# Tile 1 of the MoE in mixed blocks: its h units all move into the third MoE stage, and two h units leave the place ahead of the third column

## The chip, the cores and the metric

The kernel runs on one core of one Trainium2 chip. The metric is the device time of one execution in microseconds (us), as a median over runs. The engines are called TensorE (PE, with PEld for its weight loads), VectorE (DVE), ScalarE (ACT), GpSimd (POOL) and SyncE (SP, which here only issues DMAs). POOL issues DMAs too.

## The reference

For each of 8 batches, attention without softmax gates `u`, and the result goes through a two-layer block with activation h·cos(h):

```python
scores = (1 / S) * z @ z.T            # z: 3008 x 64 for each batch
attn = np.maximum(scores, 0.0) ** 2
x = u * (attn @ v)                    # u, v: 3008 x 256
h = x @ w_in                          # 256 x 2048
out = (h * np.cos(h)) @ w_out         # 2048 x 256
```

Inputs and output are float32; the kernel computes in fp16 with float32 sums.

## The kernel before

The tokens of a batch are cut into 6 columns of 512 (the last has 448), so there are 48 tiles or slots, numbered by s = 6·batch + column. Each slot has two stages, and the main loop runs them in turn: `phase_a(s)` is the attention of column s, `phase_b(s)` the MoE of earlier tiles. The first three columns use `phase_a_first`. All instructions are put out in an order written by hand; each engine and each DMA queue works through its own in that order and waits on semaphores.

- **Scores** (`emit_score`, matmuls at L191): a 128x1024 block into one of three PSUM buffers E, which rotate. ScalarE takes the relu into r (L204), VectorE squares it into a piece A (L209, L212). Half of the pieces come from their mirror image by a DMA transpose on SP's queue (L244; L238 for those on the diagonal). Scores are put out ahead of need, between the value matmuls.
- **Values** (`emit_value`, L258): v times A. The first half of the features is summed in the two banks M, the second half in one buffer E. `gate_sum` copies one bank on ScalarE (L269) and adds the other on VectorE (L270); with that the bank or the buffer is free. `gate_mul` (L286) multiplies with the transposed u (uT) and gives x: the first half on VectorE inside `phase_a(s)`, the second on POOL at the head of `phase_b(s)`. In `phase_a_first` the two products of a tile are made later: those of tile 0 and 1 inside the next column on VectorE, those of tile 2 on POOL at the head of `phase_b(2)`. x has two buffers, so tile 3 takes that of tile 1.
- **h units** (`emit_h(m, i)`, i = 0 to 7): four matmuls of 512 columns (L403) into a buffer E, the cosine on ScalarE (L411, the profile's c), and h·cos(h) on VectorE (L414), which gives g and frees E. g has two buffers.
- **y, plain** (`emit_y(m, i)`, L507): eight matmuls of 256 columns into the two banks M; eight such steps make a tile. `store_y` evicts with ScalarE (L537).
- **y, mixed blocks** (`product(m, n)`, L465): a Strassen-like form with 7 products of 16 matmuls of 128 columns, in place of the 8 steps. Before it, for each of the units 4 to 7, `mix_early` on POOL makes one sum and one difference of halves of g (L427, L428), and `mix_late` on VectorE makes s2 and s4 in four operations (L433, L435) inside the next `phase_a`. After each product its bank M is taken by ScalarE (L484) or VectorE (L478). Two more sums run on POOL: c12 after product 6 (L487) and c22 after product 7 (L490). VectorE's sum after product 3 reads c12, that after product 4 writes c21, which c22 reads. `mixed(m)` says which tiles take this form. The weights for it, w_mix, are made once on POOL (L444).

`phase_b(s)` makes the h units of tile s - 1 and the y of tile s - 2, in turns: one h unit, one step or product of y. The start differs: tile 0 has four h units ahead of column 2, its others and six units of tile 1 come in `phase_b(2)`, and the last two of tile 1 open `phase_b(3)`. The order of products is

```python
order_y = (5, 1, 6, 7, 2, 3, 4)
...
acc = M[order_y.index(n) % 2][:, 0:T]
```

Around this, POOL's queue holds, in order: `hold` (a one-element copy, L345, that waits for the sums of the column), the load of u for the next tile, w_out (L684, behind the hold of column 1), then after column 2 the loads of u(3), u(4) and the first half of z of batch 1 (L118, L124), w_mix, the gating of tile 2, the mixing of `phase_b(2)` if there is any, and after `phase_b(2)` the second half of z. There is one z16 buffer, so this second load waits for the transpose of the first half (L133), which stands on SP's queue behind the transposes of A and the stores of tile 0.

Of the kernel before, what the change touches and what calls it, by code (L numbers as in the profile page):

```python
# [14 lines left out]
def kernel(  # L15
# [18 lines left out]
    CW = 512  # L34
# [4 lines left out]
    NSLOT = B * NC  # L39
# [186 lines left out]
    def emit_turns(due, more=0):  # L226
        while turns and (turns[0][0] <= due or more > 0):
            if turns[0][0] > due:
                more -= 1
            (b, c), key = turns.pop(0)  # L230
            b, J, I = key
            i = turn_slots[key]
            a = piece_bufs[i]
            if I == J:
                a4 = a.rearrange("p (k w) -> p k w", w=CW)
                for rr in range(2, 4):
                    rows = P if J * 4 + rr < NB - 1 else H
                    nc.sync.dma_start_transpose(  # L238
                        a4[:, 0:2, rr * P:rr * P + rows],
                        a[0:rows, rr * CW:rr * CW + 2 * P],  # L240
                    )
            else:
                d = new_piece((b, I, J))
                nc.sync.dma_start_transpose(d.rearrange("p (n j) -> p n j", j=P), a)  # L244
            if pending.pop(i) == "dropped":
                free_pieces.append(i)
# [26 lines left out]
    def gate_mul(s, dh, sm, eng=None):  # L273
        eng = eng or nc.vector
        J = s % NC
        b = s // NC
        W = width(J)
        if s not in xs:
            if J == NC - 1 and b % 2 == 1:
                xs[s] = xodd  # L280
            else:
                xs[s] = xpool.tile([P, 2, CW], FP16, name="x")
        x = xs[s]
        uT = uTs[s].rearrange("p (k d) j -> p k d j", d=2)
        nk = W // P
        eng.tensor_tensor(  # L286
            x[:, dh, 0:nk * P].rearrange("p (k j) -> p k j", j=P),
            sm[:, 0:nk * P].rearrange("p (k j) -> p k j", j=P),
            uT[:, 0:nk, dh, :],
            ALU.mult,  # L290
        )
        if nk < 4:
            dst = x[:, dh, nk * P:W] if b % 2 == 1 else xodd[:, dh, W:CW]
            eng.tensor_tensor(
                dst, sm[:, nk * P:W], uT[:, nk, dh, 0:W - nk * P], ALU.mult
            )
# [8 lines left out]
    def phase_a(s):  # L305
# [11 lines left out]
        for i, (dh, k) in enumerate(steps):  # L317
            if dh == 2:
                emit_value(b, J, k, 0, 0, M[0], False, True)
                emit_value(b, J, k, 1, 1, acc1[1], True, False)  # L320
                gate(s, 0, M[0], M[1])
            else:
                acc = M if dh == 0 else acc1
                last = k == NB - 2
                for t in range(2):
                    emit_value(
                        b, J, k, t, dh, acc[t],
                        k == 0 and not (dh == 1 and t == 1),
                        last and not (dh == 0 and t == 0),
                    )  # L330
                if dh == 1 and (k % 4 == 3 or last):
                    drop_piece((b, J, k // 4))
            for _ in range(at.get(i, 0)):
                emit_score()
                emit_turns(divmod(s + 1, NC), 1)
            if i in mix_at and mixed(s - 2):
                mix_late(s - 2, *mix_at[i])
# [55 lines left out]
    def mwidth(m):  # L393
        return 3 * P if m % (2 * NC) == NC - 1 else CW

    def emit_h(m, i):
        W = mwidth(m)
        x = xs[m]
        e = E[take_e()]
        for f in range(2):  # L400
            ft = 2 * i + f
            for k in range(2):
                nc.tensor.matmul(  # L403
                    e[:, f, 0:W],
                    w_in16[:, k, ft * P:(ft + 1) * P],
                    x[:, k, 0:W],
                    start=(k == 0),
                    stop=(k == 1),
                )
        c = cpool.tile([P, 2, CW], FP16, name="c")  # L410
        nc.scalar.activation(c[:, :, 0:W], e[:, :, 0:W], AF.Sin, bias=half_pi, scale=inv_s2)  # L411
        if m not in gs:
            gs[m] = gpool.tile([P, NFT, CW], FP16, name="g")
        return lambda: nc.vector.scalar_tensor_tensor(  # L414
            gs[m][:, 2 * i:2 * i + 2, 0:W], e[:, :, 0:W], 1.0, c[:, :, 0:W], ALU.mult, ALU.mult
        )

    def mixed(m):
        return 2 <= m < NSLOT - 2 and mwidth(m) == CW

    F = NFT // 2
    T = 2 * P
# [1 line left out]
    def mix_early(m, j):  # L424
        g, f = gs[m], slice(2 * j, 2 * j + 2)
        lower = slice(F + 2 * j, F + 2 * j + 2)
        nc.gpsimd.tensor_tensor(s1[:, f, :], g[:, f, T:], g[:, lower, T:], ALU.add)  # L427
        nc.gpsimd.tensor_tensor(g[:, f, T:], g[:, f, 0:T], g[:, f, T:], ALU.subtract)  # L428
# [86 lines left out]
    def emit_y(m, i):  # L515
        for ft in range(2 * i, 2 * i + 2):
            for k in range(mwidth(m) // P):
                y_block(m, ft, k)

    def store_half(m, half, o):  # L520
        b, J = m // NC, m % NC
        n = min(2, mwidth(m) // P - 2 * half)
        t0 = b * S + J * CW + half * T
        if J == NC - 1 and half == 1 and n == 2:
            nc.sync.dma_start(out[t0:t0 + P, :], o[:, 0, :])
            nc.sync.dma_start(out[t0 + P:t0 + P + H, :], o[0:H, 1, :])
            nc.sync.dma_start(out[b * S - H:b * S, :], o[H:P, 1, :])
        else:
            nc.sync.dma_start(
                out[t0:t0 + n * P, :].rearrange("(k p) d -> p k d", p=P), o[:, 0:n, :]  # L530
            )

    def store_y(m):
        for half in range(2):
            n = min(2, mwidth(m) // P - 2 * half)
            o = opool.tile([P, 2, D], FP32, name="o")
            nc.scalar.activation(  # L537
                o[:, 0:n, :],
                M[half].rearrange("p (k d) -> p k d", d=D)[:, 0:n, :],
                AF.Copy, bias=0.0, scale=inv_s2,  # L540
            )
            store_half(m, half, o)
# [22 lines left out]
    def phase_b(s):  # L565
        y, hs = s - 2, [(s - 1, i) for i in (0, 4, 1, 5, 2, 6, 3, 7)]
        if s == 2:
            hs = [(0, i) for i in range(4, 8)] + [(1, i) for i in range(6)]
        elif s == 3:
            hs = [(1, 6), (1, 7)] + hs  # L570
        elif s == NSLOT + 1:
            hs = []
        for dh in range(len(late_sums)):
            gate_mul(s, 2 - len(late_sums), late_sums.pop(0), nc.gpsimd)
        if mixed(y):
            ys = [lambda n=n: product(y, n) for n in order_y]
        else:
            ys = [lambda i=i: emit_y(y, i) for i in range(8)]
            if len(hs) == 8:
                six, seven = ys[6:]  # L580
                ys[6:] = [lambda: (six(), seven(), store_y(y))]
            else:
                ys[7] = lambda f=ys[7]: (f(), store_y(y))
        n = 0
        for i, (m, unit) in enumerate(hs):
            times_c = emit_h(m, unit)
            if not mixed(y):
                times_c()
            if i < len(ys):
                ys[i]()  # L590
            if mixed(y):
                times_c()
            if mixed(m) and unit >= 4:
                mix_early(m, unit - 4)
            if i in (1, 3, 5):
                emit_turns((0, 0), 1)
# [85 lines left out]
    phase_a_first(0, 12, {4: lambda: turn_late(4), 8: lambda: turn_late(5)})  # L682
    phase_a_first(1, 12)
    nc.gpsimd.dma_start(w_out16, moe_w_out.rearrange("(k p) f -> p k f", p=P))  # L684
    for i in range(4):
        emit_h(0, i)()
    phase_a_first(2, 14)
    assert done_groups[0] == need[3]
# [3 lines left out]
    load_z(1, 0)  # L692
    mix_weights()
    phase_b(2)
    turn_z(1, 0)
    load_z(1, 1)
# [56 lines left out]
```

## Time and profile before

| | us |
|---|---|
| median of 3 runs | 1202.3 |
| lowest and highest | 1202.19, 1202.38 |
| profiled execution | 1201.01 |
| its span | 1199.2 |
| TensorE busy (matmuls) | 1188.9 |
| VectorE, ScalarE, POOL busy | 989.6, 796.2, 642.9 |

The granted TensorE clock of the profiled run is 0.999 of full speed. The stages at the start lie as follows in its span, by the first TensorE instruction of each: `phase_a_first(2)` 41.90, `phase_b(2)` 56.20, `phase_a(3)` 72.47, `phase_b(3)` 83.78, `phase_a(4)` 101.65, `phase_b(4)` 113.52, `phase_a(5)` 126.78. In a timeline row the columns are start, length, engine, line, operation, output <- input, count, and in brackets the idle time of that engine before it with what ended it. A waits row gives total us, times, longest.

### The profile page before, as it was taken

What the parts mean: (1) busy time and instruction counts of PE and PEld (TensorE: products, weight loads), DVE (VectorE), ACT (ScalarE), POOL (GpSimd) and SP (SyncE); (2) the same over time, 40 slices, a digit from 0 to 9 for tenths busy, and PEclk for the clock granted to TensorE, in tenths of its full rate; (3) what the DMA queues carried; (4) which work ended last, traced back from release to release, by engine and by line L of the source; (5) the groups of instructions that cost most, each with busy time, mean ns of one, the idle gap of its engine ahead of it and who ended that gap; (6) DMA issues with size and microseconds to landing.
All of it is one profiled execution on the core that took longest, in us unless ns stands there. A gap on an engine that the chain in (4) does not pass through costs nothing.

```text
span 1199.2 us, 28321 instructions
## 1 busy us (share of the span) xinstructions
PE 1188.9 (99%) x11695; PEld 703.2 (59%) x11695; DVE 989.6 (83%) x1248; ACT 796.2 (66%) x923; POOL 642.9 (54%) x657
## 2 busy tenths in 40 slices
PE   9999999999999999999999999999999999999998
PEld 4455655665556655665556655665556555666566
DVE  6858888888988887788988889788888888878775
ACT  7957666666766666666766676666766667666444
POOL 3155735567555571665746656166565765525440
PEclk9999999999999999999999999999999999999999
DMA  9999898869997589946999569983798837964301
GB/s 158 167 165 147 126 154 114 122 102 132 131 124 121 105 135 158 129 80 119 140 145 132 82 111 148 165 114 76 113 163 149 117 71 117 172 112 89 62 19 54
DMA packets 467410, 145.13 MB, mean 121 GB/s; under 512 B 391760, under 2 KB 467024, under 8 KB 467280
## 3 DMA queue, kind: packets, MB, share of 16 engines
q1 hardware_dynamic: 368304, 110.11, 52.8%
q0 software_dynamic: 97440, 32.78, 28.7%
q8 instruction: 91, 1.49, 0.5%
q10 hardware_dynamic: 1536, 0.43, 0.2%
q14 instruction: 39, 0.32, 0.1%
HBM read 66.32 MB, written 24.64 MB: 76 GB/s over the span
## 4 chain that ended last, share of the span: by engine, by line
PE 96%; ACT 1%; DVE 1%; issue 1%; DVEq 0%; ACTq 0%
PE E L403 27%; PE M L465 21%; PE M L258 20%; PE E L258 19%; PE E L191 5%; PE M L507 4%; ACT r L204 1%; DVE g L414 0%; PE E L636 0%; DVE A L209 0%; DVE sm L270 0%; DVE A L212 0%; PE E L507 0%; DVE x L286 0%; PE M L660 0%
## 5 line engine op out<-in xcount | busy, mean ns | idle before, releaser
L411 ACT ACTIVATE c<-E 128x1024 f16<-128x1024 f32 (+1 forms) x384 | 386.0, 1007 | 223.8 <-PE E L403 222.9
L414 DVE SCALAR_TENSOR_TENSOR g<-E,c 128x1024 f16<-128x1024 f32 (+1 forms) x384 | 458.9, 1197 | 77.5 <-ACT c L411 77.0
L204 ACT ACTIVATE r<-E 128x512 f16<-128x512 f32 (+1 forms) x342 | 327.9, 967 | 114.8 <-PE E L191 109.9
L258 PEld LDWEIGHTS <-v 64*128 64x128 f16 x4512 | 225.3, 94 | 252.3 <-issue 19.2
L403 PE MATMUL E<-x,w_in 128*128 128x512 f16 (+1 forms) x1408 | 354.3, 374 | 2.7 <-DVE sm L270 2.0
L258 PE MATMUL M<-A,v 64*128 64x512 f16 (+1 forms) x2256 | 282.9, 372 | 0.3 <-DVE sm L270 0.3
L427 POOL TENSOR_TENSOR s<-g 128x512 f16<-128x512 f16 x160 | 187.2, 1170 | 174.4 <-DVE g L414 132.6
L258 PE MATMUL E<-A,v 64*128 64x512 f16 (+1 forms) x2256 | 278.0, 372 | 0.0
L428 POOL TENSOR_TENSOR g<-g 128x512 f16<-128x512 f16 x160 | 198.2, 1239 | 12.6
L403 PEld LDWEIGHTS <-w_in 128*128 128x128 f16 x1536 | 134.6, 98 | 112.4 <-issue 22.7
L209 DVE TENSOR_TENSOR A<-r 128x1024 f16<-128x1024 f16 x240 | 172.6, 730 | 21.3 <-ACT r L204 20.6
L286 POOL TENSOR_TENSOR x<-sm,uT 128x512 f16<-128x512 f32 (+1 forms) x43 | 48.5, 1130 | 244.8 <-DVE sm L270 244.6
L465 PEld LDWEIGHTS <-g 128*128 128x128 f16 x2560 | 156.4, 98 | 36.1
L465 PEld LDWEIGHTS <-s 128*128 128x128 f16 x1920 | 117.3, 98 | 27.1
L191 PE MATMUL E<-zT 64*128 64x512 f16 (+2 forms) x684 | 126.6, 363 | 2.0 <-DVE zT L631 1.1
L433 DVE TENSOR_TENSOR s<-s,g 128x1024 f16<-128x1024 f16 x80 | 90.9, 1137 | 2.1 <-POOL s L427 2.1
L212 DVE TENSOR_TENSOR A<-r 128x512 f16<-128x512 f16 (+1 forms) x102 | 77.0, 756 | 15.0 <-ACT r L204 14.5
L465 PE MATMUL M<-w_out,g 128*128 128x128 f16 x1280 | 84.5, 219 | 0.0
L465 PE MATMUL M<-w_mix,s 128*128 128x128 f16 x1280 | 84.5, 219 | 0.0
L465 PE MATMUL M<-w_mix,g 128*128 128x128 f16 x1280 | 84.5, 219 | 0.0
L191 PEld LDWEIGHTS <-zT 64*128 64x128 f16 x684 | 35.7, 94 | 41.8 <-issue 4.1
L507 PE MATMUL M<-w_out,g 128*128 128x256 f16 x432 | 55.8, 273 | 0.4 <-DVE sm L270 0.4
(55 smaller groups left out, 685.6 us busy)
## 6 DMA issues: line engine op xcount, KB each, us to landing
out_dram<-o SPq DMA_DIRECT2D x87, 256.0 KB, 2.2
v<-in_v_dram POOLq DMA_DIRECT2D x40, 256.0 KB, 9.3
u<-in_u_dram POOLq DMA_DIRECT2D x40, 256.0 KB, 4.8
A<-A SPq DMA_TRANSPOSE x207, 5.4
z<-in_z_dram POOLq DMA_DIRECT2D x14, 192.0 KB, 11.3
z<-in_z_dram POOLq DMA_DIRECT2D x14, 176.0 KB, 6.0
v<-in_v_dram POOLq DMA_DIRECT2D x8, 192.0 KB, 12.2
u<-in_u_dram POOLq DMA_DIRECT2D x8, 192.0 KB, 4.0
```

The source lines that it names most:

```text
L191: nc.tensor.matmul(e[:, t, 0:W], zT[t * H:(t + 1) * H, k * P:(k + 1) * P], zT[t * H:(t + 1) * H, J * CW:J * CW + W], start=True, stop=True,)
L204: nc.scalar.activation(r[:, :, 0:W], e[:, :, 0:W], AF.Relu)
L209: nc.vector.tensor_tensor(a4, r4, r4, ALU.mult)
L258: nc.tensor.matmul(bank[:, 0:width(J)], vs[b, k // 4][t * H:(t + 1) * H, k % 4, dh * P:(dh + 1) * P], value_rhs(b, J, k, t), start=start, ...
L403: nc.tensor.matmul(e[:, f, 0:W], w_in16[:, k, ft * P:(ft + 1) * P], x[:, k, 0:W], start=(k == 0), stop=(k == 1),)
L411: nc.scalar.activation(c[:, :, 0:W], e[:, :, 0:W], AF.Sin, bias=half_pi, scale=inv_s2)
L414: return lambda: nc.vector.scalar_tensor_tensor(gs[m][:, 2 * i:2 * i + 2, 0:W], e[:, :, 0:W], 1.0, c[:, :, 0:W], ALU.mult, ALU.mult)
L427: nc.gpsimd.tensor_tensor(s1[:, f, :], g[:, f, T:], g[:, lower, T:], ALU.add)
L428: nc.gpsimd.tensor_tensor(g[:, f, T:], g[:, f, 0:T], g[:, f, T:], ALU.subtract)
L433: nc.vector.tensor_tensor(s2[:, f, :], s1[:, f, :], g[:, f, 0:T], ALU.subtract)
L465: nc.tensor.matmul(acc[:, k * P:(k + 1) * P], left[:, ft, k * P:(k + 1) * P], right[:, ft, :], start=(ft == 0 and k == 0), stop=(ft == F - ...
L507: nc.tensor.matmul(y_bank(m, k), gs[m][:, ft, k * P:(k + 1) * P], w_out16[:, ft, :], start=(ft == 0 and (k % 2 == 0 or (final and k == 3)) ...
```

## The change

Tile 1 joins the tiles that take mixed blocks. All eight of its h units stand in `phase_b(2)`, in the order 0, 4, 1, 5, 2, 6, 3, 7 in which the other tiles have theirs, behind h(0,2) to h(0,7). Only h(0,0) and h(0,1) stay ahead of `phase_a_first(2)`. With 14 h units there, the eight y steps of tile 0 follow the h units with the indices 1, 2, 4, 5, 7, 8, 10, 11 (counted from 0). `phase_b(3)` has the eight units of tile 2 alone, and the seven products of tile 1. For the other stages the new list of places gives the order that they had.

```diff
     def mixed(m):
-        return 2 <= m < NSLOT - 2 and mwidth(m) == CW
+        return 1 <= m < NSLOT - 2 and mwidth(m) == CW
...
         y, hs = s - 2, [(s - 1, i) for i in (0, 4, 1, 5, 2, 6, 3, 7)]
         if s == 2:
-            hs = [(0, i) for i in range(4, 8)] + [(1, i) for i in range(6)]
-        elif s == 3:
-            hs = [(1, 6), (1, 7)] + hs
-        elif s == NSLOT + 1:
-            hs = []
+            hs = [(0, i) for i in range(2, 8)] + hs
...
             ys = [lambda i=i: emit_y(y, i) for i in range(8)]
-            if len(hs) == 8:
-                six, seven = ys[6:]
-                ys[6:] = [lambda: (six(), seven(), store_y(y))]
-            else:
-                ys[7] = lambda f=ys[7]: (f(), store_y(y))
-        n = 0
+            ys[7] = lambda f=ys[7]: (f(), store_y(y))
+        n = len(hs)
+        if n > 8:
+            after = (1, 2, 4, 5, 7, 8, 10, 11)
+        elif mixed(y):
+            after = range(7)
+        else:
+            after = (0, 1, 2, 3, 4, 5, 6, 6)
         for i, (m, unit) in enumerate(hs):
             times_c = emit_h(m, unit)
             if not mixed(y):
                 times_c()
-            if i < len(ys):
-                ys[i]()
+            for f, place in zip(ys, after):
+                if place == i:
+                    f()
             if mixed(y):
                 times_c()
...
-    for i in range(4):
+    for i in range(2):
         emit_h(0, i)()
     phase_a_first(2, 14)
```

## The prediction, made before the result was known

> **What bounds the kernel now.** I read the page's busy times first, then the waits of TensorE, then the timeline around the places that the diff touches, then two stretches side by side.
>
> ```profile
> PE 1188.9 (99%) x11695; PEld 703.2 (59%) x11695; DVE 989.6 (83%) x1248; ACT 796.2 (66%) x923; POOL 642.9 (54%) x657
> ...
> PE E L403 <- DVE sm L270: 2.0, 1, 2.0
> PE E L403 <- DVE g L414: 0.7, 1, 0.7
> PE E L191 <- DVE g L414: 0.5, 1, 0.5
> PE M L507 <- DVE sm L270: 0.4, 1, 0.4
> ```
>
> TensorE works 99% of the span, and nearly all of its waits after the first 15 us are these four, each happening once, all before 90 us. So only two things can make this kernel shorter: fewer matmul columns, or the loss of one of these waits. The largest, 2.0 us, is here:
>
> ```profile
> 85.53 1.03 PE L403 MATMUL E<-x,w_in 128*128 128x512 f16 x4
> 86.59 0.69 DVE L286 TENSOR_TENSOR x<-sm,uT 128x512 f16<-128x512 f32 x1 [6.82 <-PE E L403]
> 88.67 0.68 DVE L270 TENSOR_TENSOR sm<-E,sm 128x512 f32<-128x512 f32 x1
> 89.41 1.02 PE L403 MATMUL E<-x,w_in 128*128 128x512 f16 x4 [1.98 <-DVE sm L270]
> ```
>
> [...] The gating product of tile 3 (L286, in phase_a(3)) stands 6.82 us on VectorE and starts just as the matmuls of h(1,7) end. The x pool has two buffers, tile 3 takes that of tile 1, and before the change tile 1 is read by h(1,6) and h(1,7), which come only in phase_b(3). Behind it on VectorE queue three squares and the sum L270, which frees the E buffer for the third h unit. That unit starts at 89.41; at the pace of its neighbours (85.53 follows 83.78 by 1.75) it would start at 87.27. The loss is 2.15 us.
>
> **The change, part by part.** h(0,2) and h(0,3) leave the place ahead of the third column; with h(1,6) and h(1,7) from phase_b(3) they join phase_b(2). That is 4 units of 0.867 us (half of the 1.735 us period of h plus y), moved and not removed: 2 out, 4 in, 2 out.
>
> *Ahead of and in the third column.*
>
> ```profile
> 39.67 4.62 DVE L414 SCALAR_TENSOR_TENSOR g<-E,c 128x1024 f16<-128x1024 f32 x4
> 43.21 0.39 PE L191 MATMUL E<-zT 64*128 64x512 f16 x2 [0.49 <-DVE g L414]
> 43.64 12.83 ACT L204 ACTIVATE r<-E 128x1024 f16<-128x1024 f32 x14 [0.61 <-PE E L191]
> 44.34 0.39 PE L191 MATMUL E<-zT 64*128 64x512 f16 x2
> ```
>
> The second score at 44.34 starts when the fourth g is done (39.67 + 4.62 = 44.29). After it ScalarE's 14 relus run back to back, 12.83 us, and they, not TensorE, set the column's end. With two units there are two g of 1.155 us, done at 41.98, and the second score starts at 42.05: 2.29 us earlier. By TensorE's own work the saving would be 1.73; the other 0.56 is stall. What is late next is the M bank: the last sum L270 ahead ends at 39.66 while TensorE would arrive at 39.2, but that 0.45 us vanishes in the wait for the g. phase_b(2) starts at 56.20 - 2.29 = 53.91.
>
> *phase_b(2), 14 h and 8 y.* It lasted 16.27 us with 0.55 us of stall at the first y (L507, M bank). Now two h units stand ahead of the first y, 1.73 us, and the bank is free 1.6 us after the start (the sum on it ended at 57.79), so this stall goes. In its place comes w_out:
>
> ```profile
> w_out<-in_moe_w_out_dram POOLq DMA_DIRECT2D x1, 1024.0 KB, 15.8
> ...
> 40.39 1.16 POOL L684 DMA_DIRECT2D w_out<-in_moe_w_out_dram x1
> ...
> 57.07 0.38 PE L507 MATMUL M<-w_out,g 128*128 128x256 f16 x2
> ```
>
> It lands at 40.39 + 15.8 = 56.19. The first y used it at 57.07; now it is wanted at 53.91 + 1.73 = 55.64. I take a wait of 0.6 (ends: 0, and 1.4 if it landed as late as 57.07). The stage becomes 16.27 - 0.55 + 3.47 + 0.6 = 19.79. Two h in a row need three E buffers: one is free 3.35 us after its unit starts (matmuls, 1.02 cosine, 1.22 g, with gaps), 3.7 for the second of a pair, and its turn comes after three h and one or two y, 3.5 to 4.3 us; the second of a pair gets the longer turn. No stall. phase_a(3) starts at 73.70, 1.23 later than before.
>
> *phase_a(3) with the new mixing of tile 1.* POOL gets eight adds of 1.15 us (pairs take 2.35), VectorE four subtractions of 0.68. POOL is busy with w_mix and the gating of tile 2 until about 71.9 (0.8 us earlier than before, since the load of u(4) still waits for its buffer), so the eight end at about 81.5, 0.4 more with contention. VectorE waits there for the second s2 part until 82, and comes to the last sum L270 at 87.3 to 87.9. The third h of phase_b(3) needs that sum at 85.0 + 3.5 = 88.5. Hidden, with 0.6 us to spare. If POOL were 1.5 us later, TensorE would wait 0.9. I take 11.31 us as before; phase_b(3) starts at 85.01.
>
> *phase_b(3): y(1) of mixed blocks, 8 h.*
>
> ```profile
> 83.78:101.65 17.87, 15.89 (x107) 10.09 (x106) 12.28 (x13) 10.25 (x12) 12.18 (x15) 1.00 1.19 141
> ...
> 113.52:126.78 13.26, 13.26 (x146) 9.29 (x145) 11.10 (x15) 8.30 (x10) 7.86 (x8) 1.00 0.81 152
> ```
>
> The first column after the window is its length, the second TensorE's busy time. The first is phase_b(3), the second phase_b(4), which has exactly the new form, with no stall. 17.87 becomes 13.26: 1.73 are the units moved, 2.15 the stall on x, and 0.73 the blocks, 7 products of 0.888 instead of 8 y of 0.867. [...] This trace has 16 such matmuls in 0.888 us, 55.5 ns each, in phase_b(4), and I take that.
>
> *POOL's queue in phase_b(3) is the new wait.*
>
> ```profile
> 86.28 1.15 POOL L118 DMA_DIRECT2D z<-in_z_dram x1 [13.64 <-DMA zT<-z]
> ...
> 92.48 1.23 POOL L286 TENSOR_TENSOR x<-sm,uT 128x512 f16<-128x512 f32 x1
> ...
> 124.34 0.42 DVE L478 SCALAR_TENSOR_TENSOR o<-M,o 128x256 f32<-128x256 f32 x1 [0.27 <-PE M L465]
> 126.10 0.42 DVE L478 SCALAR_TENSOR_TENSOR o<-M,o 128x256 f32<-128x256 f32 x1 [0.20 <-PE M L465]
> ```
>
> POOL stands until 86.28 for the transpose of z(1,0), which frees the one z16 buffer; then it issues the second half of z and u(5), and is free at 92.48. That transpose hangs on SP's queue, full from 32 to 95 us, so I leave it where it is. The eight mixing adds, now ahead of it on POOL, end at 82 and don't delay it. After 92.48 come the gating (to 93.66), the first mixing pair of tile 2 (to 96.0), then the add of c12 (0.74, to 96.7) and of c22 (97.4). VectorE's sum for product 3 reads c12: its matmuls end at 95.6, so it waits for POOL until 96.8. Behind it: the g of the sixth h (1.21), then the sum of product 4, which frees bank M[0] at 98.8. phase_a(4) wants M[0] at 85.01 + 13.26 = 98.27. TensorE waits 0.55.
>
> **Sum:** -2.29 + 3.52 - 4.61 + 0.55 = -2.83 us at the start of phase_a(4) (98.82 instead of 101.65). From there on no stage has a TensorE wait to speak of and nothing else is edited, so the shift stays. Against the profiled execution of 1201.01 (span 1199.2) that is 1198.2; the median 1202.3 lies 1.3 above it, and I move it by the same: 1199.5.
>
> **The rivals.**
> *POOL is free earlier (15%).* If the transpose of z(1,0) lands 0.6 us or more sooner, bank M[0] costs nothing: -3.4, 1198.9. For it: u(3) is loaded 2 us sooner, relieving the DMA queues later. Against: those run full there (DMA share 1.16 to 1.46 of what 16 engines hold).
> *More is given back (25%).* POOL is freed 1 to 2.5 us later, or w_out and VectorE's 0.6 us of room in phase_a(3) fail together. -1.8 to -0.3, around 1201.1. For it: two margins of half a microsecond. Against: TensorE's lateness ahead of 98.3 is absorbed by the wait for M[0], so such losses don't add.
> *The stall on x doesn't go (4%).* If L286 waited for something else than h(1,7), 2.15 us stay: -0.7, 1201.6. Against: it starts 0.03 us after that unit's matmuls, and no later tile shows it.
> *Slower (6%).* One mechanism: POOL's wait for zT. Each microsecond that the transpose of z(1,0) lands later than 86.28 is one on M[0], since c12 hangs on it. Before the change no TensorE work hung on it. The median passes +0.2% from 5.2 us later on. One transposition of A in that queue takes up to 6.5 us; one more ahead of it gives -2.83 + 6.5 = +3.7, 1206.0. Against: the order on SP is unchanged.
> The main case holds 50%: 1199.5, own range 1199.1 to 1199.9.
>
> **How the numbers follow.** 0.2% is 2.4 us, about what a measurement of this kernel can tell from no change. Faster by more than that: the main case (allowing a tenth of it for -2.3), the early POOL, a little of the third: 0.62. Within: 0.32. Slower: 0.06. The range 1198.6 to 1201.6 leaves out the slower case, the end of the given-back one, and something better than -3.7.
>
> **What would show it.** Right: no L286 wait of several us on VectorE near 80; second score near 42; a wait of TensorE at the first L507 for w_out near 56; phase_a(4) at about 98.8 with a wait of M (L258) on VectorE's L478, and POOL's L487 starting near 96. Wrong: a TensorE wait at the third h of phase_b(3) (VectorE late after mixing), products longer than 0.89 us, POOL's L118 at another time than 86, or a new wait after 105 us.

## The result, and the profile after

| | before | after |
|---|---|---|
| median, us | 1202.24 (4 runs) | 1197.62 (4 runs) |
| lowest and highest | 1200.84, 1202.38 | 1197.28, 1198.03 |
| ratio | | 0.9964 (0.9947 to 0.9982) |
| profiled execution, its span | 1201.01, 1199.2 | 1197.28, 1195.5 |

The forecast was 1199.5 with a range from 1198.6 to 1201.6. The direction held and the kernel became faster than the range allowed: by 4.6 us in the medians, by 3.7 in the profiled executions. Why these two numbers differ is the subject of the larger part of what follows. A repeat with more runs gave 1197.89 against 1200.95, ratio 0.9973 (0.9962 to 0.9985); one of its six runs took 1199.93, 1.9 us above the next, and stands in no profile.

The waits of TensorE after the change:

```profile
PE E L635 <- DVE s L598: 1.2, 1, 1.2
PE E L191 <- DVE zT L630: 1.1, 1, 1.1
PE E L191 <- DVE g L414: 0.4, 1, 0.4
PE M L258 <- DVE sm L270: 0.3, 1, 0.3
```

Of the four waits shown of before, the 2.0 on L270, the 0.7 ahead of column 2 and the 0.4 at the first y are gone. The first two rows here belong to the start and were there before. The stages from phase_b(2) to phase_a(4), as windows (the 1.00 near the end of a row is TensorE's granted clock):

```profile
53.78:72.96 19.18, 19.18 (x122) 11.65 (x121) 16.29 (x16) 14.46 (x18) 16.92 (x14) 1.00 1.38 178
72.96:84.27 11.31, 11.31 (x108) 5.08 (x107) 10.82 (x12) 7.11 (x9) 7.67 (x7) 1.00 1.11 199
84.27:97.53 13.26, 13.26 (x146) 9.29 (x145) 11.40 (x16) 8.30 (x10) 13.10 (x17) 1.00 1.24 133
97.53:109.40 11.87, 11.87 (x111) 5.27 (x111) 11.54 (x15) 9.17 (x10) 6.47 (x6) 1.00 0.81 128
```

Length and busy time are equal in all four: TensorE stands nowhere. phase_b(3) has its 13.26 us to the digit, and phase_a(4) starts at 97.53 instead of 101.65, 4.12 us earlier. The shift stays so until TensorE's last group of matmuls (1193.48 before, 1189.36 after). The timeline shows the two places where the prediction had put new waits:

```profile
83.95 1.14 POOL L118 DMA_DIRECT2D z<-in_z_dram  x1 [3.40 <-DMA zT<-z]
...
93.70 0.73 POOL L487 TENSOR_TENSOR o<-p,p 128x256 f32<-128x256 f32 x1
...
95.09 0.42 DVE L478 SCALAR_TENSOR_TENSOR o<-M,o 128x256 f32<-128x256 f32 x1 [0.27 <-PE M L465]
...
97.53 0.82 PE L258 MATMUL M<-A,v 64*128 64x512 f16 x6
```

POOL got its z buffer at 83.95, not 86.28, so the sum c12 (L487) ended at 94.43. VectorE's sum for product 3 asked for it at 95.09, and its bracket names the product's matmuls, not POOL. And w_out:

```profile
w_out<-in_moe_w_out_dram POOLq DMA_DIRECT2D x1, 1024.0 KB, 14.2
```

Issued at 40.22, it landed at 54.42, ahead of the first y at 55.52.

### The profile page after: what moved, and what is told of

Read it like the earlier page. It is cut to its first block, busy times and chain, and to the rows that moved or that the text cites. A ratio compares the mean times of both kernels' runs of the same rounds, so it can differ in the third digit from the quotient of the medians.

```text
span 1195.5 us, 28444 instructions
## 1 busy us (share of the span) xinstructions
PE 1187.7 (99%) x11743; PEld 703.3 (59%) x11743; DVE 996.6 (83%) x1257; ACT 795.7 (67%) x923; POOL 654.6 (55%) x667
## 4 chain that ended last, share of the span: by engine, by line
PE 97%; ACT 1%; DVE 1%; issue 0%; DMA 0%; DVEq 0%; ACTq 0%; SPq 0%
PE E L403 27%; PE M L465 21%; PE M L258 20%; PE E L258 19%; PE E L191 6%; PE M L507 3%; ACT r L204 1%; PE E L635 0%; DMA out_dram<-o 0%; DVE g L414 0%; DVE sm L270 0%; ACT o L554 0%; DVE A L212 0%; DVE A L209 0%; PE turned L620 0%
## 5 line engine op out<-in xcount | busy, mean ns | idle before, releaser
L427 POOL TENSOR_TENSOR s<-g 128x512 f16<-128x512 f16 x164 | 192.6, 1174 | 171.2 <-DVE g L414 131.8
L428 POOL TENSOR_TENSOR g<-g 128x512 f16<-128x512 f16 x164 | 203.4, 1240 | 12.9
L209 DVE TENSOR_TENSOR A<-r 128x1024 f16<-128x1024 f16 x240 | 173.5, 734 | 20.6 <-ACT r L204 19.8
L286 POOL TENSOR_TENSOR x<-sm,uT 128x512 f16<-128x512 f32 (+1 forms) x43 | 48.6, 1131 | 244.5 <-DVE sm L270 244.3
L465 PEld LDWEIGHTS <-g 128*128 128x128 f16 x2624 | 160.3, 98 | 37.0
L465 PEld LDWEIGHTS <-s 128*128 128x128 f16 x1968 | 120.2, 98 | 27.7
L433 DVE TENSOR_TENSOR s<-s,g 128x1024 f16<-128x1024 f16 x82 | 93.2, 1137 | 2.1 <-POOL s L427 2.1
L212 DVE TENSOR_TENSOR A<-r 128x512 f16<-128x512 f16 (+1 forms) x102 | 78.4, 769 | 13.7 <-ACT r L204 12.7
L435 DVE TENSOR_TENSOR s<-g,s 128x1024 f16<-128x1024 f16 x82 | 56.0, 685 | 0.0
```

What stands on the lines that cost most here:

```text
L209: nc.vector.tensor_tensor(a4, r4, r4, ALU.mult)
L212: nc.vector.tensor_tensor(a4, r[:, :, 0:W], r[:, :, 0:W], ALU.mult)
L433: nc.vector.tensor_tensor(s2[:, f, :], s1[:, f, :], g[:, f, 0:T], ALU.subtract)
L465: nc.tensor.matmul(acc[:, k * P:(k + 1) * P], left[:, ft, k * P:(k + 1) * P], right[:, ft, :], start=(ft == 0 and k == 0), stop=(ft == F - ...
```

## The experiments

Times are medians, ratios against runs of the kernel before on the same chip. The expectations are quoted as put down ahead of each run.

**The kernel before again, three times.** No edit.

> The kernel before once more, unchanged: how much do its own DMA times move between executions? Theory: the two waits that the prediction counted and that did not come (first y on w_out, bank M[0] on POOL) hang on DMA times that differ from run to run by a microsecond or more; then w_out's 15.8 us to landing and the moment when POOL gets its z buffer back (86.28) come out differently here by 1 us or more, while TensorE's four waits and the span (1199.2) stay within 0.4 us. Rival: the change itself made these DMAs earlier; then this run repeats 15.8 and 86.3 within 0.3 us.

> The kernel before, unchanged, for a profile of the upper group of its times (near 1202.3, against 1200.9 in the three profiles so far). The kernel with its own x buffer for tile 3 had no such group in 10 runs, and the edit of the tail did not remove it, so it should lie at the stall on x or right behind it: a profile of 1202.3 shows a fifth wait of TensorE of about 1.4 us between 60 and 130 us. Rival: it lies at the start or the tail, and TensorE's waits are the same four.

> As e9_before: one more draw of the same kernel. A time near 1200.9 repeats the four waits, one near 1202.3 shows where the 1.4 us are.

Measured: 1201.04, 1202.46 and 1201.15. First, the DMA times do move with nothing changed: w_out took 15.1, 14.9 and 15.0 us to land (15.8 in the first profile) and POOL got its z buffer at 85.64, 84.90 and 84.91 (86.28). The first of these runs alone moved both by 0.6 to 0.7 us, which is between its expectation and its rival. Over the four profiles POOL's moment varies by 1.4 us and w_out by 0.9; over all the profiles of this case w_out varies more (below). The four waits stayed the same.

Second, the run of 1202.46 is one of a separate group. Of 61 timed executions of the kernel before over all comparisons, 32 lie between 1200.6 and 1201.2, 29 between 1202.0 and 1202.7, and none between. The expectation of a fifth wait was wrong, though not its place. TensorE's waits in this run are the old ones, and yet phase_b(3), from 83.51 to 103.06, takes 19.55 us instead of 17.87. Its timeline and its windows at the stall on x:

```profile
89.14 1.02 PE L403 MATMUL E<-x,w_in 128*128 128x512 f16 x4 [1.98 <-DVE sm L270]
90.00 1.86 PE L507 MATMUL M<-w_out,g 128*128 128x256 f16 x8
91.65 1.91 PE L403 MATMUL E<-x,w_in 128*128 128x512 f16 x4
93.36 1.09 PE L507 MATMUL M<-w_out,g 128*128 128x256 f16 x8
```

```profile
86.00:89.14 3.14, 1.16 (x11) 0.79 (x9) 2.82 (x6) 1.02 (x1) 3.14 (x6) 1.00 1.06 73
89.14:90.00 0.86, 0.86 (x5) 0.38 (x4) 0.86 (x1) 0.00 (x0) 0.86 (x2) 1.00 1.36 96
90.00:93.40 3.40, 3.40 (x14) 1.76 (x13) 2.48 (x3) 1.02 (x1) 2.33 (x4) 0.51 1.51 187
93.40:103.06 9.66, 9.66 (x67) 6.19 (x65) 6.12 (x5) 6.59 (x8) 4.75 (x5) 1.00 0.67 109
```

One h unit (0.86 us) after the wait of 1.98 us the granted clock is 0.51 for 3.40 us, then full again. A y step that takes 0.87 us lasts 1.65 there (90.00 to 91.65), and the h unit after it 1.71. 3.4 us at half speed cost 1.7, which is the 1.68 by which the stage is longer. (In the whole this execution lost less, since it began phase_b(3) 0.27 to 0.41 us earlier than the three others.) So the stall on x had a second price in this execution: behind it the clock was halved for 3.4 us. The clocks on record for the timed executions agree. They exist for 57 of the 61: in the lower group all 31 have a mean granted clock of 0.999 or 1.000, in the upper group 24 of 26 have 0.998 (the other two 0.999), and 3.4 us at half clock take 0.0014 off the mean over 1200 us.

The wait has nearly the same length in all six profiles that hold it (two are of kernels further below; times in us, the clock as a mean over the stretch named):

| kernel, its time | stall on x | its length | granted clock behind it |
|---|---|---|---|
| before, 1201.01 | 87.43 to 89.41 | 1.98 | 1.00 (90.00 to 96.00) |
| before, 1201.04 | 87.44 to 89.42 | 1.98 | 1.00 (90.00 to 96.00) |
| before, 1201.15 | 87.57 to 89.55 | 1.98 | 1.00 (90.00 to 96.00) |
| before with the tail edit, 1200.92 | 87.36 to 89.34 | 1.98 | 1.00 (90.00 to 96.00) |
| before, 1202.46 | 87.16 to 89.14 | 1.98 | 0.51 (90.00 to 93.40) |
| only the head, 1204.08 | 88.78 to 90.77 | 1.99 | 0.53 (91.50 to 95.00) |

Behind it the clock falls in two profiles and stays full in four. What decides between the two is not shown by these runs; by the times, 29 of the 61 executions, 48%, lie in the upper group.

**The changed kernel again.** No edit.

> The changed kernel once more, for the size of its gain on one chip. By the two profiles TensorE's work ends 4.1 us earlier (last matmul group 1193.48 to 1189.36), of which 0.2 lies ahead of the first edit, so the time should fall by 3.7 to 4.2 us, ratio about 0.9967. If the medians seen so far (4.6) are the better reading: 0.9962. If the DMA times vary, w_out lands and POOL gets its z buffer at other times than 54.4 and 83.95, and a wait of up to 0.6 us may appear at one of the two places.

1197.89 against 1200.95, ratio 0.9973 (0.9962 to 0.9985). TensorE's work ends 0.28 us later than in the first profile (the start of the kernel differs by that), again without a new wait. The medians' 4.6 us was thus not repeated: it had set the changed kernel against a median from the upper group.

**x of tile 3 in its own buffer.** Before, with one edit:

```diff
-            if J == NC - 1 and b % 2 == 1:
+            if s == 3 or (J == NC - 1 and b % 2 == 1):
                 xs[s] = xodd
```

> The kernel before, but the x of tile 3 lies in the spare x buffer instead of that of tile 1; nothing else is moved. Theory: the 6.8 us wait of L286 on VectorE and the 2.0 us wait of TensorE at the third h unit of phase_b(3) go, phase_b(3) takes 15.7 us instead of 17.87, time about 2.15 us less than before, ratio 0.9982. Rival (VectorE would be late there anyway, or POOL's late gating takes over): less than 1 us.

1198.71, ratio 0.9978 (0.9969 to 0.9987). The stage and VectorE's gating:

```profile
83.79:99.51 15.72, 15.72 (x106) 10.07 (x104) 10.49 (x9) 10.24 (x12) 12.17 (x15) 1.00 1.07 144
```

```profile
79.81 0.69 DVE L286 TENSOR_TENSOR xodd<-sm,uT 128x512 f16<-128x512 f32 x1
```

15.72 us as expected, 2.15 less, and L286 runs at 79.81 without a wait. Ten of ten runs lie between 1198.2 and 1198.9: with the stall gone, the second group is gone too. The edit touches nothing but that stall, so the second group hung on it; that it hung on it through the clock is what the profile of 1202.46 (0.51 for 3.40 us) and the clocks on record (0.998 in 24 of 26 of the upper group) show. The edit is worth 2.2 us against the lower group (mean 1200.92) and 3.6 against the upper (1202.27). It moves no h unit, so the loss of this stall alone brings the largest part of the gain.

**Tile 1 with plain y.** The changed kernel with

```diff
-        return 1 <= m < NSLOT - 2 and mwidth(m) == CW
+        return 2 <= m < NSLOT - 2 and mwidth(m) == CW
```

> The changed kernel with tile 1 left in the plain form of y; all its h units stay in the third stage. Theory: only the gain of the block form is missing, phase_b(3) takes 13.9 to 14.0 us instead of 13.26, time 0.7 us above the changed kernel and 3.3 below the one before, ratio to before 0.9973. [...] Rival 2 (mixing of tile 1 costs hidden time on VectorE and POOL): equal.

```profile
53.66:74.09 20.43, 19.36 (x123) 11.57 (x122) 16.29 (x16) 14.46 (x18) 14.37 (x11) 1.00 1.45 188
...
85.39:99.39 14.00, 14.00 (x98) 9.30 (x97) 9.26 (x8) 8.72 (x10) 13.41 (x16) 1.00 1.13 144
```

phase_b(3) takes 14.00 us against 13.26: the block form saves 0.74, as the prediction had it from products of 0.888 us in phase_b(4) of before (16 matmuls of 128 columns, 55.5 ns each). The median is 1197.7, though (ratio 0.9969, 0.9957 to 0.9981), equal to the changed kernel's within what these runs tell. The whole time is too coarse here, since the tail (below) and w_out move by as much; the stage tells. In this profile the tail's wait is 1.58 us, as before the change; against the changed kernel with the tail edit (1196.87, on another chip) the plain form is 0.8 slower. Its profile also caught the wait that the changed kernel's two had missed:

```profile
PE M L507 <- DMA w_out<-in_moe_w_out_dram: 1.1, 1, 1.1
```

In that execution w_out took 16.5 us. Over twelve profiles with the load in its old place it took 13.6 to 16.5.

**POOL later by two adds.** The changed kernel with

```diff
     def phase_b(s):
+        if s == 3:
+            for i in range(2):
+                nc.gpsimd.tensor_tensor(
+                    xodd, w_in16[:, :, 0:CW], w_in16[:, :, CW:2 * CW], ALU.add
+                )
```

> The changed kernel with two adds more on POOL (128x1024, 2.1 us each, into the spare x buffer, which nothing reads yet) at the head of phase_b(3), ahead of the gating of tile 3. Theory: POOL's sum c12 decides when bank M[0] is free; it ended 0.66 us ahead of its need (94.43 against 95.09), so 4.2 us more on POOL put 3.2 to 3.6 us of wait on M at the start of phase_a(4), and the time rises by that. Rival: POOL lies beside the path there, time as the changed kernel.

1203.09, ratio 1.0012 (1.0003 to 1.0021), 5.2 us above the changed kernel's repeat. VectorE waits for POOL, TensorE for the bank behind it, and then the clock drops:

```profile
99.03 0.42 DVE L478 SCALAR_TENSOR_TENSOR o<-M,o 128x256 f32<-128x256 f32 x1 [4.21 <-POOL o L487]
```

```profile
100.97 2.69 PE L258 MATMUL M<-A,v 64*128 64x512 f16 x12 [3.37 <-DVE o L478]
```

```profile
100.97:104.40 3.43, 3.43 (x18) 1.61 (x19) 2.21 (x2) 0.49 (x1) 3.35 (x4) 0.51 0.28 95
```

The wait is 3.4 us, inside the 3.2 to 3.6 expected, so POOL's c12 does decide on bank M[0], and the changed kernel passes it with 0.66 us to spare. The time rose by 1.8 more than the wait, which was not expected; 3.43 us at a clock of 0.51, the same price as at the stall on x, make 1.7 of it. From 104.40 to 114.53 the clock is 1.00 again.

**The tail.** In the changed kernel's profile the third of the last four evictions waits for a store, because two o buffers serve four blocks:

```profile
1191.46 0.39 ACT L554 ACTIVATE o<-M 128x256 f32<-128x256 f32 x1 [2.94 <-DMA out_dram<-o]
1191.77 0.38 ACT L554 ACTIVATE o<-E 128x256 f32<-128x256 f32 x1
```

In the kernel before this wait was 1.58 and hid behind TensorE. The edit, for both kernels:

```diff
+        os = [opool.tile([P, 2, D], FP32, name="o") for i in range(2)]
...
-            o = opool.tile([P, 2, D], FP32, name="o")
+            o = os[k // 2][:, k % 2, :]
```

> The kernel before, with the last four blocks of out in four halves of the two o buffers, so that no eviction waits for a store (in its profile the third waits 1.58 us, hidden behind the last matmuls). The kernel before has times near 1200.85 and near 1202.3 and little between. Theory: a slow store in the tail makes the upper group; then all runs come near 1200.8. Rival: the upper group comes from somewhere else; then both groups stay.

> The changed kernel with the same edit of the tail. In its two profiles the third eviction waited 2.9 and 3.4 us for a store, and the last one ended 0.4 and 0.9 us later than TensorE's end allows. Theory: that goes, 0.4 to 0.9 us less than the changed kernel, 1196.9 to 1197.2, and the runs lie closer together. Rival: the stores are as late for the last block, no change.

On the kernel before: 1201.01, ratio 0.9999 (0.999 to 1.0008), both groups still there, as the rival said. On the changed kernel: 1196.87, ratio 0.9959 (0.9947 to 0.9971), all runs between 1196.7 and 1197.0. The last eviction comes at 1191.16 instead of 1191.77. So the tail had given back 0.4 and 0.9 us of the changed kernel's gain in its two profiles. All three profiles with the whole change and the old tail have this wait at 2.9 to 3.4 us, the seven others with the old tail at 1.6. Why isn't settled.

**Only the head of the change.** The kernel before with

```diff
-            hs = [(0, i) for i in range(4, 8)] + [(1, i) for i in range(6)]
+            hs = [(0, i) for i in range(2, 8)] + [(1, i) for i in range(6)]
...
-    for i in range(4):
+    for i in range(2):
         emit_h(0, i)()
```

> The kernel before with only the head of the change: two h units ahead of column 2, the other two first in phase_b(2), which has 12 units; y of tile 0 follows from the first on, tile 1 is finished in phase_b(3) as before. Theory: ahead of phase_b(2) 2.25 us go, 1.73 come back, gain 0.5; but y asks for w_out 0.9 us sooner than in the changed kernel, at 54.7, where it lands between 54.0 and 56.9 by the profiles so far, so 0 to 2.2 us of wait take its place, and the net is between 0.5 less and 1.7 more. The wait on x stays. Rival (order of h units costs nothing): equal.

1202.86, ratio 1.001 (1.0001 to 1.0019): slower. Seven of its ten runs have a granted clock of 0.998, a larger share than in the kernel before, so part of this is the halved clock; the three others, 1201.5 to 1202.6, still lie above the lower group. Column 2 gives up its 0.5 us of stall (phase_b(2) starts at 53.77), but then the first y waits for w_out, which took 16.0 us, and the four h units in a row at the end of the stage wait for E:

```profile
56.28 1.05 PE L507 MATMUL M<-w_out,g 128*128 128x256 f16 x8 [1.48 <-DMA w_out<-in_moe_w_out_dram]
72.88 1.02 PE L403 MATMUL E<-x,w_in 128*128 128x512 f16 x4 [0.80 <-DVE g L414]
90.77 1.02 PE L403 MATMUL E<-x,w_in 128*128 128x512 f16 x4 [1.99 <-DVE sm L270]
```

The stall on x stays, and in this profile it too is followed by half clock (table above). The whole change asks for w_out one h unit later and spreads the y steps over the 14 units; neither was tried by itself.

**Two attempts to go further.** The changed kernel with the tail edit and w_out loaded ahead of column 1; and the same with the second diff on top.

```diff
+    nc.gpsimd.dma_start(w_out16, moe_w_out.rearrange("(k p) f -> p k f", p=P))
     phase_a_first(1, 12)
-    nc.gpsimd.dma_start(w_out16, moe_w_out.rearrange("(k p) f -> p k f", p=P))
```

```diff
-    on_dve = ()
+    on_dve = (34,)
```

> The changed kernel with the tail edit, and the load of w_out put out ahead of column 1 instead of behind it (13 us earlier, behind the hold of column 0). Theory: w_out lands by 45 us and the first y can never wait for it (it waited 1.07 and 1.48 us in two of the kernels with y that early, 0 in four); median as with the tail edit alone, 1196.9, since that kernel waited in none of its five runs, or up to 0.3 less. Rival: the load comes between the transposes of column 1 and costs more there (a wait of TensorE on A or x near 30 us): 1 us or more slower.

> The same as e11_w_early, and one of the 14 relus of column 2 done on VectorE. In the changed kernel ScalarE works 15.54 of that stretch's 16.47 us and TensorE 15.93, so up to 0.5 us could go. Theory: 0.3 to 0.5 us less than e11. Rival: VectorE (13.75 of 16.47, then 15) falls behind with the squares and the g, no gain or a loss of up to 1 us.

The first: 1196.73, ratio 0.9958 (0.9945 to 0.9972), the best time here, though not to be told from the tail edit alone (1196.87). w_out landed in 12.9 us, at 39.6, 16 us ahead of the first y at 55.80. The second: 1198.57, ratio 0.9975 (0.9964 to 0.9985), 1.8 us slower than the first:

```profile
PE E L191 <- DVE r L202: 1.7, 1, 1.7
```

The relu on VectorE stands in its queue behind the two gating products and a square, so its E buffer comes free late, and the score that wants it waits 1.70 us. No fall of the clock follows this one (1.00 from 50.00 to 56.00), and the eight runs lie within 0.4 us.

## Why the prediction was wrong in size and right in direction

The forecast lies 1.88 us above the measured median. Of this, 0.92 is in the profiled execution (1198.2 put, 1197.28 measured), and 0.96 in the step from there to the median (1.3 put, 0.34 measured). Term by term:

- *Ahead of and in column 2.* Put at -2.29. From the first h unit to phase_b(2) it took 18.72 us before (37.48 to 56.20) and 16.47 after (37.31 to 53.78): -2.25. Right.
- *phase_b(2).* Put at +3.52; it was 19.18 against 16.27, +2.91. The E buffers held, and the wait on M went. The term that failed is w_out's 0.6: 0 in the profiles of the changed kernel, 1.07 and 1.48 in two kernels near it. I had taken one execution's 15.8 us for a constant; it belongs to a spread from 13.6 to 16.5. The bounds of 0 and 1.4 held for the changed kernel; that the wait came to 0 there is luck of the draw.
- *phase_a(3).* 11.31 as put. VectorE's last sum started at 85.63 and TensorE wanted it at 87.79; hidden, with more room than the 0.6 us given. The 0.4 us for contention were an estimate; in the profile after, the last two of POOL's eight adds took 1.60 and 1.48 us against 1.15 of the first, and three operations on VectorE between 76.34 and 81.11 (L433, L212, L209) 1.64 each, where L433 and L209 took 0.68 and 0.69 later in the stage.
- *phase_b(3).* Put at -4.61 in three parts, measured 17.87 to 13.26, -4.61. The stall on x and the blocks were each confirmed alone (2.15, 0.74).
- *Bank M[0].* Put at +0.55, was 0. The chain from POOL to the bank is real (two adds more on POOL gave 3.4 us of wait); the mistake was to leave POOL's moment at 86.28. Over the twelve profiles with the load of w_out in its old place it was 83.95 to 84.43 in the four that hold the whole change, and 84.72 to 86.28 in the eight others. So 86.28 was a late draw, and with the change the moment came about 1 us earlier on top (means 84.2 and 85.3). What goes with it is the load of z(1,0), here before and after:

```profile
59.85 2.05 POOL L118 DMA_DIRECT2D z<-in_z_dram  x2
...
57.55 2.03 POOL L118 DMA_DIRECT2D z<-in_z_dram  x2
```

  The prediction had POOL only 0.8 us earlier here, "since the load of u(4) still waits for its buffer". In the profiles of the changed kernel it did not wait, and POOL was 2.3 us earlier. Over all fourteen profiles POOL's moment is 83.80 to 84.43 in the five where this load starts by 57.9, and 84.72 to 86.28 in the nine where it starts at 59.3 or later. The second attempt to go further has the whole change and is among the nine (59.31 and 84.90); so are the plain form and the head alone, where u(4) did wait. No run moved this load by itself, so the link is a correlation, and the cause stays open.
- *The sum.* -2.83 put, -4.12 measured on TensorE at phase_a(4): 0.61 from w_out, 0.55 from M[0], 0.17 from a start that was earlier ahead of any edit, less 0.04 at the head. The rival "POOL is free earlier" (1198.9) was the case that came, with w_out early on top; its reason, that the earlier u(3) relieves the DMA queues, was not tried by itself.
- *The end.* "The shift stays" held for TensorE; the tail gave back 0.4 of it in this profile.
- *From the profiled execution to the median.* This step failed worst: the median "lies 1.3 above it, and I move it by the same". The 1.3 was no constant around the program. It was the halved clock after the stall on x (0.51 for 3.40 us in the profile of 1202.46), which the profile of before had not caught, and which goes with the stall. Without it the kernel before runs at about 1200.9, and the change brings 3.0 to 3.3 us (1200.92 to 1197.89 or 1197.62); with it, another 1.35. The signal was on the table: three unprofiled runs at 1202.2 to 1202.4 and the profiled one at 1201.0.

## What to carry to other kernels

Where times fall into two tight groups and the profile fits only one, look for what the other group adds before moving the median by a constant: in this kernel a wait of TensorE of 1.98 us was followed, in two of the six profiles that hold it, by a granted clock of about half (0.51 for 3.40 us in one). Removing this wait, which by itself had cost 2.15 us, brought 3.6 us against the upper group, and it drew the runs together: with the own x buffer all ten lie within 0.7 us. A DMA's landing time from one profile is one draw (w_out took 13.6 to 16.5 us here): give it a spread, and prefer a change that asks for the data later, or loads them earlier, to one that lands inside the spread.

## What was not expected of the hardware

TensorE's granted clock fell to about half for some 3.4 us behind a wait of TensorE of 1.98 us in the profile of 1202.46 (0.51 from 90.00 to 93.40), of 1.99 us in that of only the head (0.53 from 91.50 to 95.00) and of 3.37 us in that of POOL later (0.51 from 100.97 to 104.40). It stayed at 1.00 behind the wait of 1.98 us in the four other profiles of the table, and behind waits of 1.70 us (a relu on VectorE), 1.48 us (w_out, only the head) and 1.07 us (w_out, plain y). What decides it is not shown by these runs. The third eviction of the tail waited 1.6 us for its store in the kernel before and 2.9 to 3.4 in the changed one, with the tail's code unchanged; that was not explained.
